# First mixture of a clustered-attention chain: weights bounded in place on VectorE, a fourth raw buffer, one block sum by accumulating DMA, one output block added by VectorE, and a new order of the steps

## The chip, the cores and the metric

The kernel runs on one core of one Trainium2 chip. The metric is device time in microseconds (us) of one execution of the whole program. All engine names are those of the profile: PE is TensorE (PEld its weight load), DVE VectorE, ACT ScalarE, POOL GpSimd, SP SyncE, which here only issues DMAs.

## The reference

Three layers run one after the other. The change touches the second.

```python
attn_out = _attn_ref(q, k, v, centroids)              # clustered attention, 2 x 8 heads, 768 x 64
x = attn_out.transpose(0, 2, 1, 3).reshape(1536, 512)
h = x @ w_in                                          # "first mixture": 512 -> 2048
g = h * (1.0 / (1.0 + np.exp(-h)))
x = g @ w_out                                         # 2048 -> 512
return _moe2_ref(x, w_gate, w1, w2)                   # 8 experts, weighted by a balanced gate
```

`w_in` and `w_out` come in float64, everything else that matters here in float32.

## The kernel before

**The first mixture** works in four stages `s`, each for 512 of the 2048 hidden columns. A stage has two layers, and each layer is one matrix product done as seven half-size block products with sums of blocks before and after. So a stage has 14 products: 0 to 6 are the A layer (x times w_in, PSUM tiles `l`), 7 to 13 the B layer (hidden values times w_out, tiles `y`). In the last stage the B layer is done plainly, as twelve output tiles (`ytile`, L803), because its results go straight to the third layer. Every float32 product is three PE passes: each operand is split into a rounded part `hi` and a rest `lo`.

For each product of a stage the other engines must do, in time:

- the weight factor: `mhi` (ACT casts a block of `win` or `win2` to `vh`, L150) and `mlo` (DVE subtracts, `vl`, L154). `vh` and `vl` alternate between two buffers, so those of product i can be written only when product i-2 is done;
- `aevac` (PSUM to the hidden block `h`: ACT copies or SiLU, L712 and L714; DVE adds, L716), `gsilu` (L721), `hsum` (DVE differences of hidden blocks, L753), `hhi` and `hlo` (ACT and DVE split the operand of a B product into `gh`, L759 and L763);
- `bevac` (B results): ACT copies PSUM to one of five output buffers (`rest`, `outx`, `stay`, L789), and POOL issues a DMA that adds the buffer to `acc1` (L791). The first stage's first result for each block is copied straight to `acc1`;
- `sums1`, `sum4`, `sum3`, `bsums1`, `bsum4`, `bsum3`: DVE sums of weight blocks.

**The weights** come in 32 pieces, numbered 4n + k; n = 2s is w_in and n = 2s + 1 is w_out of stage s. A piece is 512 KB: SP loads it raw into one of three buffers of pool `rawp` (`w_raw`, L86), as low and high 32-bit words. `w_steps` makes float32 of it: `wb` scales the low words (POOL, L107), `w0` scales the high words (ACT, L108; for one piece of each w_in set `wg` does that on POOL, L109), `w1` bounds the result (POOL, L110), `w2` and `w3` shift and join the bits (DVE, L111 and L112) and write the block of `win` or `win2`. In the last stage `w3` writes into the raw buffer, and `wh` and `wp2` split it into `woh` and `wol` (L113, L114). The next load into a buffer is issued when `w3` (in the last stage `wp2`) of the piece three places earlier has been issued.

**The order** is written out by hand. `put(s, u, f)` files a step under slot u of stage s; the main loop emits slot u's steps and then product u. Every engine works its own list strictly in that order, so a step that waits holds up all behind it on its engine, and POOL's list holds conversion steps and DMA issues together.

Of the kernel before, what the change touches and what calls it, by code (L numbers as in the profile page):

```python
# [18 lines left out]
P = 128  # L19
# [20 lines left out]
def attention_moe_kernel(ctx, tc, kq, vp, cent, w_in, w_out, w_gate, w1, w2, out):  # L40
# [31 lines left out]
    raws = {}  # L72
# [8 lines left out]
    def w_raw(n, k):  # L81

        raw = rawp.tile([P, 2 * FB], U32, name=f"wr{n}_{k}", tag="wr")
        shape = [P, 4, P, 2] if n % 2 == 0 else [P, 1, FB, 2]
        t = raw.rearrange("p (t f two) -> p t f two", t=shape[1], two=2)
        nc.sync.dma_start(out=t, in_=w_piece(n, k).bitcast(U32).rearrange("p t (f two) -> p t f two", two=2))  # L86
        raws[n, k] = t

    def w_steps(n, k, a=None):
# [13 lines left out]
        if 4 * n + k > 5:  # L103
            ts, v, top = nc.gpsimd.tensor_scalar, high.bitcast(F32), 122879.9921875 * 2.0**-112
            stt = nc.vector.scalar_tensor_tensor
            return dict(
                wb=lambda: ts(out=low, in0=low, scalar1=2.0**-29, scalar2=7.0, op0=ALU.mult, op1=ALU.min),  # L107
                w0=lambda: nc.scalar.activation(v, v, AF.Copy, scale=2.0**-112),  # L108
                wg=lambda: ts(out=v, in0=v, scalar1=2.0**-112, scalar2=1.0, op0=ALU.mult, op1=ALU.mult),  # L109
                w1=lambda: ts(out=v, in0=v, scalar1=-top, scalar2=top, op0=ALU.max, op1=ALU.min),  # L110
                w2=lambda: stt(out=low, in0=high, scalar=3, in1=low, op0=ALU.logical_shift_left, op1=ALU.bitwise_or),  # L111
                w3=lambda: stt(out=ai, in0=high, scalar=0x80000000, in1=low, op0=ALU.bitwise_and, op1=ALU.bitwise_or),  # L112
# [538 lines left out]
    wop = pool(rctx, "wop", bufs=1, side="right")  # L651
    mps = pool(rctx, "mps", bufs=6, space=PSUM)
# [4 lines left out]
    rest = wop.tile([P, 2048], F32, name="rest", tag="wol")  # L657
    wsum2 = rest[:, :512].rearrange("p (k f) -> p k f", k=2)
    outs = [rest[:, 512 + i * S : 512 + (i + 1) * S] for i in range(2)]
# [78 lines left out]
    BX = {1: (0, 1), 5: (0, 1), 6: (0, 1), 3: (1, 0), 7: (0, 0), 2: (1, 1), 4: (1, 1)}  # L738
# [3 lines left out]
    def bsums1():  # L742
        nc.vector.tensor_tensor(out=b21, in0=b21, in1=b22, op=ALU.add)
        nc.vector.tensor_tensor(out=wsum2, in0=b21, in1=b11, op=ALU.subtract)

    def bsum4():
        nc.vector.tensor_tensor(out=b21, in0=b12, in1=wsum2, op=ALU.subtract)

    def bsum3():
        nc.vector.tensor_tensor(out=b11, in0=b22, in1=wsum2, op=ALU.subtract)  # L750
# [26 lines left out]
    def bevac(s, j, pieces=PIECES):  # L777
# [4 lines left out]
        straight = s == 0 and p in (1, 5, 6, 4)  # L782
        if not straight and (s, j) not in moved:
# [15 lines left out]
    def ytile(s, t):  # L799
        c, d = CHUNKS[t // 4], t % 4  # L800
        ps = banks[t] = (mpy if t in (0, 1, 10, 11) else mps).tile([P, 512], F32, name=f"y{s}_{t}", tag="y" if t in (0, 1, 10, 11) else "s")
        def go(out, w, k, g, first=False, last=False):
            nc.tensor.matmul(out, lhsT=w[:, k, d * P : (d + 1) * P], rhs=g, start=first, stop=last, skip_group_check=True)  # L803
# [477 lines left out]
    def narrow(n, k, keys):  # L1281
# [3 lines left out]
        for key in keys.split():  # L1285
            quarters[n, k][key](*((wo_h[:, k : k + 1], wo_l[:, k : k + 1]) if key in ("wh", "wp2") else ()))
# [4 lines left out]
    LASTN = 2 * NS1 - 1  # L1291

    def bring(k):
        steps.pop(k + 4)
        nc.scalar.copy(win2[:, k : k + 1, :], raws[1, k][..., 1].bitcast(F32))
        w_raw(1 + (k + 3) // 4, (k + 3) % 4)

    X, Y, Z, V = (0, 1), (0, 0), (1, 0), (1, 1)
    for s in range(NS1):
        n, first, last = 2 * s + 1, s == 0, s == NS1 - 1  # L1300
        done = ("w2 w3 wh", "wp2") if last else ("w2 w3", "")
# [4 lines left out]
        def finish(u, k):  # L1306
            go(u, narrow, n, k, done[0])

        if not first:
            go(0, bevac, s - 1, 6)  # L1310
        go(0, mhi, s, 1)
        go(0, mlo, s, 1)
# [3 lines left out]
        else:  # L1316
            go(0, narrow, n - 1, 3, "w2 w3")
            go(0, sums1)
            go(0, narrow, n, 0, "w0 w1 wb")
        go(1, aevac, s, 0)  # L1320
        go(1, mhi, s, 2)
        go(1, mlo, s, 2)
        go(1, sum4)
        go(1, sum3)
        if first:
            go(1, split, 7, xb)
            go(1, narrow, n, 2, "w0 w1 wb")
        else:
            go(1, narrow, n, 1, "w0 w1 wb")
# [3 lines left out]
        if not first:  # L1333
            finish(2, 0)
            go(2, narrow, n, 2, "w0 w1 wb")
        go(2, gsilu, 2)
        go(3, aevac, s, 2)
        go(3, mhi, s, 4)
        go(3, mlo, s, 4)
        if not first:  # L1340
            if last:
                go(3, narrow, n, 0, done[1])
            finish(3, 1)
        else:
            go(3, split, 4, xd)
            go(3, narrow, n, 3, "w0 w1 wb")
        if last:
            go(3, ghi, 2)
        else:
            for m in range(2):  # L1350
                go(3, hhi, 0, m)
            for m in range(2):
                go(3, hlo, 0, m)
        go(4, aevac, s, 3)
        go(4, mhi, s, 5)
        go(4, mlo, s, 5)
        if last:
            go(4, narrow, n, 1, done[1])
        finish(4, 2)
        if last:  # L1360
            go(4, narrow, n, 2, done[1])
        if not first:
            go(4, narrow, n, 3, "w0 w1 wb")
        go(5, aevac, s, 4)
        go(5, mhi, s, 6)
        go(5, mlo, s, 6)
        go(5, gsilu, 7)
        finish(5, 3)
        go(6, aevac, s, 5)
        if last:  # L1370
            go(6, ghi, 7)
            go(6, narrow, n, 3, done[1])
# [16 lines left out]
        go(6, narrow, n + 1, 1, "w0 w1 wb")  # L1389
        go(7, bsums1)  # L1390
# [391 lines left out]
```

## Time and profile before

| | us |
|---|---|
| median of 3 runs | 1453.52 (1452.60 to 1454.64) |
| profiled execution, own time | 1451.86 |
| its span, first to last instruction | 1450.1 |
| around the span | 1.76 |

Busy shares of the span: PE 98%, PEld 88%, DVE 82%, ACT 70%, POOL 34%. The granted TensorE clock was 0.999 of full speed on average. In the page's 40 slices of 36 us, attention is the first six and a half, the first mixture lies from there to about the fourteenth, and the rest is the third layer. How to read it: a share over the whole span mixes three layers with different limits, and a PE row is longer (0.28 us) than the distance to the next one (0.12 us), since matmuls overlap; what the first mixture takes is therefore read from the starts of its products.

### The profile page before, as it was taken

To read this page: it belongs to the slowest core of one execution; us is meant where nothing else is said; L and a number is where in the kernel's file an instruction comes from. 1 tells how busy PE (TensorE), PEld (TensorE's weight loads), DVE (VectorE), ACT (ScalarE), POOL (GpSimd) and SP (SyncE) were. 2 spreads that over 40 slices of the span, in tenths; PEclk is the share of its full clock that TensorE was granted. 3 is DMA by queue.
4 is the path that set the end of the run, shared out by engine and by line. 5 is a ranking of instruction groups with operands and counts; after the bars stand their busy time and mean duration, and the time that the engine had idled before them with its cause. 6 is when DMAs were issued, how large, how long until landed. Compare 5 with 4: busy or idle time off the path is not lost.

```text
span 1450.1 us, 25558 instructions
## 1 busy us (share of the span) xinstructions
PE 1414.8 (98%) x9709; PEld 1279.2 (88%) x9709; DVE 1186.0 (82%) x1926; ACT 1018.1 (70%) x1974; POOL 486.6 (34%) x428
## 2 busy tenths in 40 slices
PE   8999999999997999999999999999999999999998
PEld 5777778877775889999999999999999999999998
DVE  7788887978776898988878778788787887887878
ACT  7777777766665367658577677786776867767765
POOL 6677754576864001121322322120211202212112
PEclk9999999999999999999999999999999999999999
DMA  7665520256574018486697897867957869569587
GB/s 221 184 170 156 172 65 29 52 160 123 146 164 120 1 36 176 83 158 147 134 184 136 164 156 143 167 108 124 162 95 145 137 115 171 98 120 167 89 153 131
DMA packets 141210, 190.87 MB, mean 132 GB/s; under 512 B 6816, under 2 KB 109216, under 8 KB 141088
## 3 DMA queue, kind: packets, MB, share of 16 engines
q0 software_dynamic: 88752, 100.94, 45.1%
q1 hardware_dynamic: 51648, 87.85, 19.4%
q8 instruction: 76, 1.25, 0.3%
q10 hardware_dynamic: 688, 0.46, 0.1%
q14 instruction: 46, 0.38, 0.1%
HBM read 65.36 MB, written 88.87 MB: 106 GB/s over the span
## 4 chain that ended last, share of the span: by engine, by line
PE 65%; DVE 1%; ACT 1%; issue 0%; DVEq 0%; ACTq 0%
PE b L685 27%; PE a L685 23%; PE b L1136 4%; PE q L1116 4%; PE r L1116 4%; PE y L803 2%; DVE acc L1217 1%; PE a L1130 0%; DVE al L848 0%; PE gl L1048 0%; ACT gh L726 0%; DVE h L845 0%; ACT acc L1234 0%; DVE h L1271 0%; DVE wfl L848 0%
## 5 line engine op out<-in xcount | busy, mean ns | idle before, releaser
L685 PE MATMUL b<-wfh,ah 128*128 128x256 f32 x1164 | 330.8, 284 | 0.0
L685 PE MATMUL b<-wfh,al 128*128 128x256 f32 x1164 | 329.2, 283 | 0.0
L685 PE MATMUL b<-wfl,ah 128*128 128x256 f32 x1164 | 329.1, 283 | 0.0
L1243 POOL DMA_DIRECT2D out_dram<-acc x87 | 126.5, 1720 | 533.6 <-ACT acc L1234 510.1
L1234 ACT ACTIVATE acc<-b,Pg 128x256 f32<-128x256 f32 x564 | 222.8, 540 | 6.2 <-PE b L1136 5.2
L685 PEld LDWEIGHTS b<-wfl,ah 128*128 128x128 f32 x1164 | 223.1, 192 | 0.0
L685 PEld LDWEIGHTS b<-wfh,ah 128*128 128x128 f32 x1164 | 222.9, 191 | 0.2
L685 PEld LDWEIGHTS b<-wfh,al 128*128 128x128 f32 x1164 | 223.0, 192 | 0.0
L685 PE MATMUL a<-xfl,wfh 128*128 128x512 f32 (+1 forms) x640 | 215.8, 337 | 0.0
L685 PE MATMUL a<-xfh,wfl 128*128 128x512 f32 (+1 forms) x640 | 215.5, 337 | 0.0
L685 PE MATMUL a<-xfh,wfh 128*128 128x512 f32 (+1 forms) x640 | 215.4, 337 | 0.0
L1169 ACT CAST ah<-h 128x768 fp32r<-128x768 f32 x160 | 134.6, 853 | 110.7 <-DVE h L1265 53.3
L1156 ACT COPY h<-a 128x512 f32<-128x512 f32 x192 | 113.9, 620 | 102.1 <-PE a L685 96.1
L848 DVE TENSOR_TENSOR al<-h,ah 128x768 fp32r<-128x768 f32 x160 | 151.3, 954 | 28.7 <-ACT ah L1169 23.4
L685 PEld LDWEIGHTS a<-xfh,wfl 128*128 128x128 f32 x640 | 120.9, 189 | 12.9
L685 PEld LDWEIGHTS a<-xfh,wfh 128*128 128x128 f32 x640 | 121.1, 189 | 11.6 <-issue 0.6
L685 PEld LDWEIGHTS a<-xfl,wfh 128*128 128x128 f32 x640 | 121.0, 189 | 10.4
L331 ACT ACTIVATE p<-s,m 128x768 f32<-128x768 f32 x96 | 86.7, 904 | 35.2 <-DVE m L322 30.7
L348 POOL TENSOR_SCALAR p<-p,rec 128x768 f32<-128x768 f32 x95 | 86.2, 920 | 51.5 <-DVE rec L336 39.4
L322 DVE TENSOR_REDUCE m<-s 128x1 f32<-128x768 f32 x96 | 90.0, 951 | 13.9 <-PE s L315 13.5
L845 DVE TENSOR_TENSOR h<-q,h 128x384 f32<-128x384 f32 x112 | 60.9, 554 | 35.1 <-PE q L1116 32.8
L848 DVE TENSOR_TENSOR wfl<-w0r,wfh 128x512 fp32r<-128x512 f32 x96 | 64.6, 688 | 28.9 <-ACT wfh L961 28.9
(281 smaller groups left out, 3498.6 us busy)
## 6 DMA issues: line engine op xcount, KB each, us to landing
out_dram<-acc POOLq DMA_DIRECT2D x91, 768.0 KB, 8.8
w0r<-in_w_dram SPq DMA_DIRECT2D x16, 1024.0 KB, 5.8
w1r<-in_w_dram SPq DMA_DIRECT2D x16, 1024.0 KB, 8.4
qk<-qk SPq DMA_DIRECT2D x45, 192.0 KB, 3.5
wr<-in_w_in_dram SPq DMA_DIRECT2D x16, 512.0 KB, 4.0
wr<-in_w_out_dram SPq DMA_DIRECT2D x16, 512.0 KB, 6.5
first_out<-acc POOLq DMA_DIRECT2D x10, 768.0 KB, 8.8
raw<-in_kq_dram SPq DMA_DIRECT2D x16, 384.0 KB, 4.1
```

The costliest lines, as they stand in the source:

```text
L322: nc.vector.tensor_reduce(out=m, in_=tiles[i]["s"][:, :S], axis=AX.X, op=ALU.max, negate=True)
L331: nc.scalar.activation(t["p"], t.pop("s")[:, :S], AF.Exp, bias=t.pop("m"), accum_out=chunks[c]["sum"][:, j, 0:1])
L348: e.tensor_scalar(out=p, in0=p, scalar1=chunks[c]["rec"][:, j : j + 1], scalar2=1.0, op0=ALU.mult, op1=ALU.mult)
L685: nc.tensor.matmul(ps[u][:, cols], lhsT=lf(i, k), rhs=rt(j, k), start=fresh and u not in opened, stop=k == 1 and q == 2, skip_group_check= ...
L845: e.tensor_tensor(out=out, in0=in0, in1=in1, op=op)
L848: e.tensor_tensor(out=lo, in0=x, in1=r(hi), op=ALU.subtract)
L1116: nc.tensor.matmul(ps, lhsT=quad_lhs(s, q, a, four), rhs=(x4 if four else xq)[b][:, XQ[q]], start=j == 0 and q in (1, 2, 5), stop=j == 2, ...
L1136: nc.tensor.matmul(ps[u][:, cols], lhsT=lf(i, k), rhs=rt(j, k), start=u not in opened, stop=k == 1 and q == 2, skip_group_check=True)
L1156: act.copy(bank(t, u), ps[u])
L1169: act.copy(hi, x)
L1234: act.mul(t[:, 2 * u + m], z[:, m], Pg[:, 6 * i + 2 * u + m, e : e + 1])
L1243: gps.dma_start(out=to, in_=t, accum_op=ALU.add)
```

## The change

- `w1` becomes a VectorE instruction (`clamp`) for all pieces but those of the last stage. `w0` writes the scaled high words straight into the place of `win` or `win2` (ACT for every piece; `wg` is gone), and `w1`, `w2`, `w3` work there; `wb` multiplies by a constant a little smaller and has no bound any more.
- A fourth raw buffer `rxp` takes the pieces 7, 11, 15, 19, 23 and 27, and loads are issued four pieces ahead. Piece 7 is loaded as soon as the buffer is there. `rest` becomes shorter, `wsum2` and the last `wol` block move.
- The signs of some sums change, so that one hidden block is a sum: `fourth` adds block (1,1) to block (0,1) by one accumulating DMA of 768 KB on POOL's queue. It takes the place of two DVE `hsum` instructions in each of the first three stages, and the last B product reads block (0,1).
- `bevac` of B product 12 (p = 2) is four DVE instructions that add PSUM to `acc1`, in place of four ACT copies and two DMAs.
- The lists are laid out anew: among others `mhi` stands ahead of the evacuations, the operand splits are interleaved by halves, and the conversion of the last piece of a w_in set (`w1 w2 w3`) follows directly before `sums1`.

```diff
+        raw = (rxp[0] if 4 * n + k in (7, 11, 15, 19, 23, 27) else rawp).tile([P, 2 * FB], U32, name=f"wr{n}_{k}", tag="wr")
...
-            ts, v, top = nc.gpsimd.tensor_scalar, high.bitcast(F32), 122879.9921875 * 2.0**-112
-            stt = nc.vector.scalar_tensor_tensor
+            ts, top = nc.gpsimd.tensor_scalar, 122879.9921875 * 2.0**-112
+            stt, clamp = nc.vector.scalar_tensor_tensor, ts if n == LASTN else nc.vector.tensor_scalar
             return dict(
-                wb=lambda: ts(out=low, in0=low, scalar1=2.0**-29, scalar2=7.0, op0=ALU.mult, op1=ALU.min),
-                w0=lambda: nc.scalar.activation(v, v, AF.Copy, scale=2.0**-112),
-                wg=lambda: ts(out=v, in0=v, scalar1=2.0**-112, scalar2=1.0, op0=ALU.mult, op1=ALU.mult),
-                w1=lambda: ts(out=v, in0=v, scalar1=-top, scalar2=top, op0=ALU.max, op1=ALU.min),
+                wb=lambda: ts(out=low, in0=low, scalar1=0.9374 * 2.0**-29, scalar2=1.0, op0=ALU.mult, op1=ALU.mult),
+                w0=lambda: nc.scalar.activation(a, high.bitcast(F32), AF.Copy, scale=2.0**-112),
+                w1=lambda: clamp(out=a, in0=a, scalar1=-top, scalar2=top, op0=ALU.max, op1=ALU.min),
...
+    def fourth():
+        nc.gpsimd.dma_start(out=hblk[0, 1], in_=hblk[1, 1], accum_op=ALU.add)
...
+        if p == 2:
+            for u, a, b, m, c in pieces:
+                z = to[:, m, c : c + b - a]
+                nc.vector.tensor_tensor(out=z, in0=ps[u][:, a:b], in1=z, op=ALU.add)
+            return
...
-            m = 4 * n + k + 3
-            if key == ("wp2" if n == LASTN else "w3") and 6 < m < 8 * NS1:
+            m = 4 * n + k + 4
+            m = {31: 32, 32: 31}.get(m, m)
+            if key == ("wp2" if n == LASTN else "w3") and m < 8 * NS1:
                 w_raw(m // 4, m % 4)
...
+        go(0, mhi, s, 1)
...
+            go(0, bevac, s - 1, 6)
+            go(0, narrow, n - 1, 3, "w1 w2 w3")
             go(0, sums1)
-            go(0, narrow, n, 0, "w0 w1 wb")
+        go(0, mlo, s, 1)
...
+        low(2, 0)
+        piece(2, 2, "w0")
+        piece(2, 3, "w0")
...
         go(2, gsilu, 2)
+        go(3, mhi, s, 4)
         go(3, aevac, s, 2)
...
-        go(11, hsum, V, V, X, m)
+        go(9, fourth)
```

How the lists moved, at the two places where stages meet or end. Rows are instructions in the order in which the engine works them; `wr_3_4825` and `wr_3_4511` are raw piece 27, `wr_0_4799`, `wr_1_4842`, `wr_2_4882` and `wr_3_5008` raw pieces 28 to 31 in the changed kernel.

ACT, from the third to the fourth stage, before: `vh_4876` and `vh_4922` are the weight parts of the fourth stage's products 0 and 1.

```order
L150 CAST vh_4876<-win 128x512
L108 ACTIVATE wr_3_4825<-wr_3_4825 128x512
L789 COPY rest<-y_2_1_4842 128x256 x2
L789 COPY rest<-y_2_0_4841 128x512
L789 COPY rest<-y_2_2_4843 128x512
L789 COPY outx<-y_1_1_4582 128x256
L789 COPY stay<-y_1_1_4582 128x256
L789 COPY outx<-y_1_0_4581 128x512
L789 COPY stay<-y_1_2_4583 128x512
L150 CAST vh_4922<-win 128x512
```

ACT at the same place in the changed kernel: `vh_4872` and `vh_4913` are the same two parts.

```order
L150 CAST vh_4872<-win 128x512
L109 ACTIVATE win<-wr_3_4511 128x4x128
L150 CAST vh_4913<-win 128x512
L799 COPY rest<-y_1_1_4583 128x256
L799 COPY outx<-y_1_1_4583 128x256
L799 COPY rest<-y_1_0_4582 128x512
L799 COPY outx<-y_1_2_4584 128x512
L109 ACTIVATE wr_0_4799<-wr_0_4799 128x512
```

Four copies (`rest<-y_2`) have left the list, and the other four stand behind the cast of product 1.

DVE at the same place in the changed kernel: the four additions to `acc`, the rest of the conversion with the bound (L110), the block sums (L135, L136) and the lo parts of products 0 and 1.

```order
L791 TENSOR_TENSOR acc_3466<-y_2_1_4846,acc_3466 128x256 x2
L791 TENSOR_TENSOR acc_3466<-y_2_0_4845,acc_3466 128x512
L791 TENSOR_TENSOR acc_3466<-y_2_2_4847,acc_3466 128x512
L154 TENSOR_TENSOR vl_4873<-win,vh_4872 128x512
L111 SCALAR_TENSOR_TENSOR wr_2_4472<-win,wr_2_4472 128x512
L112 SCALAR_TENSOR_TENSOR win<-win,wr_2_4472 128x4x128
L110 TENSOR_SCALAR win<-win 128x4x128
L111 SCALAR_TENSOR_TENSOR wr_3_4511<-win,wr_3_4511 128x512
L112 SCALAR_TENSOR_TENSOR win<-win,wr_3_4511 128x4x128
L135 TENSOR_TENSOR win<-win 128x2x256
L136 TENSOR_TENSOR wsum<-win 128x512
L154 TENSOR_TENSOR vl_4914<-win,vh_4913 128x512
```

Before, the additions were not in this list, L110 was POOL's, and the lo part of product 1 stood ahead of the conversion of piece 27.

ACT in the last stage of the changed kernel, behind the hi part of product 3 (`vh_5003`): `wr_3_5008` is the last raw piece, L723 the SiLU of a hidden block, `vh_5040` the hi part of product 4.

```order
L150 CAST vh_5003<-win 128x512
L109 ACTIVATE wr_2_4882<-wr_2_4882 128x512
L109 ACTIVATE wr_3_5008<-wr_3_5008 128x512
L723 ACTIVATE h_1_4960<-h_1_4960 128x768 x2
L150 CAST vh_5040<-win 128x512
L714 COPY h_6_5043<-l_1_0_4886 128x512
```

Before, the scaling of the last raw piece stood behind the hi part of product 5, directly ahead of that of product 6.

## Rows read from the trace of the kernel before

**Rows 1.** Windows, by stage: busy us of each engine (count), granted clock, DMA share, GB/s.

```profile
core 0: us, PE busy (x) PEld busy (x) DVE busy (x) ACT busy (x) POOL busy (x), PEclk, DMA share, GB/s
...
294.40:359.70 65.30, 60.57 (x336) 51.48 (x336) 54.19 (x69) 44.30 (x83) 47.34 (x29) 1.00 0.56 130
359.70:426.70 67.00, 61.58 (x336) 51.38 (x336) 53.37 (x69) 44.15 (x82) 48.45 (x31) 1.00 0.64 145
...
590.00:1430.00 840.00, 840.00 (x5959) 804.68 (x5958) 691.74 (x1096) 611.15 (x1210) 168.56 (x128) 1.00 0.76 137
```

**Rows 2.** Timeline of PE: first matmuls of products (start us, us, instruction, idle before).

```profile
233.18 0.50 PE L685 MATMUL l<-yh,vh 128*128 128x512 f32 x1
262.52 0.40 PE L685 MATMUL y<-gh,vh 128*128 128x256 f32 x2
276.28 0.40 PE L685 MATMUL y<-gh,vl 128*128 128x512 f32 x1
280.52 0.40 PE L685 MATMUL y<-gh,vl 128*128 128x512 f32 x1
294.47 0.50 PE L685 MATMUL l<-yh,vh 128*128 128x512 f32 x1 [0.50 <-ACT rest L789]
359.73 0.50 PE L685 MATMUL l<-yh,vh 128*128 128x512 f32 x1 [0.18 <-ACT outx L789]
426.74 0.51 PE L685 MATMUL l<-yh,vh 128*128 128x512 f32 x1 [0.18 <-ACT rest L789]
466.56 0.50 PE L803 MATMUL y<-gh,woh 128*128 128x512 f32 x1 [0.76 <-ACT gh L726]
```

**Rows 3.** Waits of PE from 233 to 502.1 us: total us, times, longest.

```profile
PE l L685 <- ACT vh L150: 10.1, 8, 2.4
PE y L685 <- DVE vl L154: 4.7, 5, 1.5
PE y L803 <- ACT gh L726: 2.2, 2, 1.5
```

**Rows 4.** Timeline of ACT: steps that waited, ahead of a late hi part.

```profile
298.54 0.68 ACT L108 ACTIVATE wr<-wr 128x512 f32<-128x512 f32 x1 [1.10 <-DMA wr<-in_w_out_dram]
...
363.71 1.35 ACT L789 COPY stay<-y 128x256 f32<-128x256 f32 x3 [2.65 <-DMA acc<-stay]
364.94 0.64 ACT L150 CAST vh<-win 128x512 fp32r<-128x512 f32 x1
```

**Rows 5.** Groups by line and form, 233 to 502.1 us: count, busy us, mean ns, idle before.

```profile
L110 POOL TENSOR_SCALAR wr<-wr 128x512 f32<-128x512 f32 x26 | 58.0, 2232 | 42.7 <-ACT wr L108 41.8
...
L753 DVE TENSOR_TENSOR h<-h,h 128x768 f32<-128x768 f32 x24 | 23.2, 1005 | 0.0
L716 DVE TENSOR_TENSOR h<-l,h 128x512 f32<-128x512 f32 x36 | 22.5, 681 | 0.0
L721 ACT ACTIVATE h<-h 128x768 f32<-128x768 f32 x24 | 18.9, 837 | 12.0 <-DVE h L716 12.0
```

**Rows 6.** Timelines of POOL and DVE: conversion steps side by side and alone, DMA issues.

```profile
312.85 2.31 POOL L107 TENSOR_SCALAR wr<-wr 128x512 uint32<-128x512 uint32 x1
...
313.21 1.14 DVE L111 SCALAR_TENSOR_TENSOR wr<-wr 128x512 uint32<-128x512 uint32 x1
321.50 0.69 DVE L111 SCALAR_TENSOR_TENSOR wr<-wr 128x512 uint32<-128x512 uint32 x1
...
427.46 1.77 POOL L791 DMA_DIRECT2D acc<-rest  x2 [3.71 <-ACT rest L789]
```

**Rows 7.** Instructions of line L120, a bound on VectorE in attention: ns min/median/max.

```profile
L120 DVE TENSOR_SCALAR u<-u x6: 418/418/548, 59.9 to 196.2; 128x512 f32<-128x512 f32 x6
```

**Rows 8.** DMA issues: KB each, median us to landing; last, raw weight loads from 425 to 465 us.

```profile
acc<-rest POOLq DMA_DIRECT2D x14, 384.0 KB, 6.8
out_dram<-acc POOLq DMA_DIRECT2D x91, 768.0 KB, 8.8
acc<-first_out SPq DMA_DIRECT2D x4, 768.0 KB, 13.6
...
DMA to landing us min/median/max: 3.6/8.5/9.9
```

More of the change, by code (lines that the diff above doesn't have):

```diff
@@ L656, in attention_moe_kernel @@
     win2 = wop.tile([P, 4, 512], F32, name="win2", tag="woh")
[L657 to L659 removed]
+    rest = wop.tile([P, 2, S], F32, name="rest", tag="wol")
+    wsum2 = wip.tile([P, 2, FB // 2], F32, name="wsum2", tag="ut")
+    outs = [rest[:, i] for i in range(2)]
     outs.append(pool(mctx, "outp", bufs=1).tile([P, S], F32, name="outx"))
@@ L802, in go @@
         def go(out, w, k, g, first=False, last=False):
-            nc.tensor.matmul(out, lhsT=w[:, k, d * P : (d + 1) * P], rhs=g, start=first, stop=last, skip_group_check=True)
+            nc.tensor.matmul(out, lhsT=w[k][:, 0, d * P : (d + 1) * P], rhs=g, start=first, stop=last, skip_group_check=True)
         if c < 2:
@@ L1300, in attention_moe_kernel, with piece, low @@
         n, first, last = 2 * s + 1, s == 0, s == NS1 - 1
-        done = ("w2 w3 wh", "wp2") if last else ("w2 w3", "")
+        mine = [k for k in range(4) if not first or k > 1]
         def go(u, f, *args):
             put(s, u, f, *args)
[L1306 to L1310, printed above, removed]
+        def piece(u, k, keys):
+            if k in mine:
+                go(u, narrow, n, k, keys)
+        def low(u, k):
+            if last:
+                go(u, narrow, n, k, "wp2")
         go(0, mhi, s, 1)
-        go(0, mlo, s, 1)
         if first:
@@ L1332, in attention_moe_kernel @@
         go(2, mlo, s, 3)
-        if not first:
-            finish(2, 0)
-            go(2, narrow, n, 2, "w0 w1 wb")
+        low(2, 0)
+        piece(2, 2, "w0")
+        piece(2, 3, "w0")
+        piece(2, 1, "w1")
+        piece(2, 3, "wb")
         go(2, gsilu, 2)
+        go(3, mhi, s, 4)
         go(3, aevac, s, 2)
-        go(3, mhi, s, 4)
         go(3, mlo, s, 4)
[L1340 to L1344, printed above, removed]
+        if first:
             go(3, split, 4, xd)
-            go(3, narrow, n, 3, "w0 w1 wb")
+        piece(3, 1, "w2 w3")
+        piece(3, 2, "w1 w2 w3")
         if last:
-            go(3, ghi, 2)
+            go(3, narrow, n, 1, "wh")
+            go(3, narrow, n, 2, "wh")
+        low(3, 1)
+        go(4, mhi, s, 5)
+        go(4, aevac, s, 3)
+        piece(4, 3, "w1 w2 w3")
+        go(4, mlo, s, 5)
+        low(4, 2)
+        if last:
+            go(4, narrow, n, 3, "wh")
+            go(4, ghi, 2)
+            go(4, glo, s, 2)
         else:
             for m in range(2):
[L1351 to L1363, printed above, removed]
+                go(4, hhi, 0, m)
+                go(4, hlo, 0, m)
+        go(5, mhi, s, 6)
         go(5, aevac, s, 4)
-        go(5, mhi, s, 6)
         go(5, mlo, s, 6)
+        low(5, 3)
+        if not last:
+            go(5, narrow, n + 1, 0, "w0")
         go(5, gsilu, 7)
-        finish(5, 3)
         go(6, aevac, s, 5)
```

107 lines of the change are left out of this document (58 added, 49 removed).

## The prediction

> **What bounds the kernel now.** I read the windows by stage first, then the starts of products on PE, then PE's waits, then the lists of the engines that PE waits for. From 590 to 1430 us PE is busy 840.00 of 840.00 us, at a granted clock of 1.00 [rows 1]. So nothing behind the first mixture can hide time that the mixture saves: each microsecond saved there moves the end by one. Inside the mixture a floor comes from the starts of products [rows 2]. The first A layer took 262.52 - 233.18 = 29.34 us for seven products. Two consecutive B products started 280.52 - 276.28 = 4.24 us apart, and seven of them take 29.68. An unstalled stage is 59.0 us. The real stages took 61.29, 65.26 and 67.01 us (the four starts), 2.3, 6.2 and 8.0 over the floor. The last stage's A layer took 466.56 - 426.74 = 39.82, 10.5 over 29.34. The plain output tiles waited another 2.2 [rows 3]. Together **29.2 us are lost**, and that is the most the change can win. The waits that the trace lists are fewer (10.1 on ACT's hi parts, 4.7 on DVE's lo parts, 2.2 on `gh` [rows 3]), because each stall also hides some of the overlap between matmul rows; I therefore count by starts.
>
> Why the hi parts are late stands in ACT's list: at 363.71 a `stay` copy waited 2.65 us for the DMA that empties an output buffer, at 298.54 a `w0` waited 1.10 us for a raw load, and the cast of the next hi part comes right behind [rows 4]. POOL spends 2.23 us on each bound [rows 5] and up to 2.31 on each `wb` [rows 6], 16 of them a stage, some 36 us, and the block sums wait at the end of that list. DVE is busy 54.2 and 53.4 us of the stages of 65 and 67 us [rows 1]: near the floor, but below it.
>
> **The change part by part**, for stages of 59.0 us.
>
> *POOL* loses eight bounds a stage (8 x 2.23 = 18 us), keeps eight `wb`, and is no longer late for the block sums in the first three stages. In the last stage it keeps its bounds.
>
> *DVE* gains eight bounds of one operand. The same form in attention took 418 ns, 548 at most [rows 7]; the two-operand conversion step took 0.69 [rows 6] and is the upper end. I take 0.42, since it is the same operation on the same tile shape: 3.4 us. It gains four additions from PSUM, two of 512 columns at 0.68 [rows 5] and two of 256, between 0.34 and 0.68; I take 0.42, some 2.2 in all. It loses two differences of 1.0 [rows 5]. That is 54.2 + 3.4 + 2.2 - 2.0 = **57.8 us of 59.0**. A step beside POOL takes 1.14 us in place of 0.69 [rows 6]; with 16 POOL steps a stage at most 7.2 us of DVE's time is such lengthening, and with eight at most 3.6, so up to 3.6 comes back: 54.2 to 57.8. DVE stays under the floor, but with little room.
>
> *ACT* loses four copies of about 0.45 (a third of 1.35 [rows 4]) and with them two output buffers to wait for; of the other four copies the hi part of the next stage's product 1 now stands ahead. It gains one `w0`, 0.68 [rows 4]. The 2.65 us wait thus no longer delays a hi part.
>
> *Stage boundaries.* Product 12 ends 4.2 us before the next stage starts. DVE then works 2.2 (additions), 0.69 (lo of product 0), 1.4 (two steps of the third piece), 0.42 + 1.4 (the last piece), 1.4 (block sums) and 0.69 (lo of product 1): 8.2 us, ready 4.0 after the start, for a product due at 4.2. One or two steps lengthened by 0.45 make it late, so I leave 1.0 lost at each of three boundaries, and 1.5 of the first stage's 2.3, whose first pieces hardly change: **4.5 us**.
>
> *Loads.* With a fourth buffer a load is issued one piece earlier; a load took 3.6 to 9.9 us [rows 8], so the 1.10 us wait goes.
>
> *The accumulating DMA.* It moves 768 KB, as the two result DMAs of 384 KB that go do. POOL issues it in 0.9 us (half of 1.77 [rows 6]) at product 9, and ACT's cast for the last B product wants it three products later, 12.6 us: 11.7 are left. The nearest rows are 6.8 us for an accumulation of 384 KB, 8.8 for 768 KB from the same queue without one, and 13.6 for 768 KB from SP's queue [rows 8]. I take 8.8, same queue and size: nothing waits. By 13.6 each of three stages would lose 1.9, 5.7 us.
>
> *The last stage* sets the rest. Let T be the start of its product 2, 8.4 us after the stage's start. ACT does a cast (0.6) and four copies (1.8), POOL two DMA issues (1.8 [rows 6]), `wb` of piece 29 and the bound of piece 28 (2.2 each): T + 0.2. DVE then needs 1.4 for `w2 w3`, 2.0 for three additions, 0.69 for the lo of product 3, 0.69 for `wp2`: T + 5.0. Only then SP loads piece 31, 3.6 us at best [rows 8]: T + 8.6. ACT's list now holds `w0` of that piece (0.68) ahead of two SiLUs (0.84 each [rows 5]) and the hi part of product 4 (0.64 [rows 4]): T + 11.6, for a product due at T + 8.4, so 3.2 are lost. Piece 31 goes on through POOL (`wb`, two bounds: T + 15.2) and DVE (1.4, the lo of product 5, `wp2`, two splits of 1.0, three additions, the lo of product 6, T + 22.7), for a product 6 due at T + 20.0: 2.7 more. The output tiles I leave 0.4. **6.3 us.**
>
> *Sum*: 29.2 - 4.5 - 6.3 = 18.4. The profiled execution took 1451.86, so 1433.5 there. The median of the runs stands 1.66 above that execution, so 1435.1 as a median.
>
> **The rivals.**
>
> *DVE becomes the bound.* If POOL's eight remaining steps fall where DVE is busiest, nothing comes back and DVE needs 57.8 us in lists with waits of their own. For it: the boundary list has 0.2 us of room. Against it: stages of 65 us had DVE at 54.2 [rows 1] and PE waited twice as long for ACT as for DVE [rows 3]. Two to four microseconds more in three stages give 1441 to 1447. Chance 0.17.
>
> *DVE waits for whole POOL steps.* A conversion step that starts beside POOL would wait, not for 0.45, but for the end of a 2.2 us step, on average 1.1. Eight steps a stage at 1.1 - 0.45 are 5.2 on top of 57.8, 63 for a floor of 59.0, 4.0 lost in each of three stages, and the same once more where the boundary list is late: about 1448. Against it stands the row of 1.14 us, which began inside a POOL step and ended inside it [rows 6]. Chance 0.05.
>
> The Trainium skill, page "SBUF — State Buffer", section "SBUF: two separate sides", states this rule: VectorE and GpSimd share a port pair as "an exclusive lock, not a bandwidth split", and the loser blocks for the whole instruction, a VectorE step with two SBUF inputs among them. It speaks against putting more on VectorE beside POOL; the trace's 1.14 against 0.69 shows a slowing and not a block, so I go by the trace.
>
> *The accumulating DMA lands late*, and the kernel ends slower. ACT works its list in order, so a cast that waits for this DMA holds the copies and the next hi parts behind it. It decides from 11.7 us after the issue; each microsecond beyond costs three. To end slower by more than a measurement of this kernel can tell from no change (0.2%, 2.9 us), it must eat the gain of 18.4 and 2.9 more, 7.1 a stage, and so land after 18.8 us. For it: DMA engines are 0.56 to 0.64 busy in these stages [rows 1], weight loads run beside it, and no row shows an accumulation of this size between two buffers of the core. Against: 13.6 is the longest near row [rows 8]. Chance 0.07, and 0.03 of it slower.
>
> *The loads gain nothing.* Buffers come free by `w3` or `wp2` on DVE, and where DVE is the later engine the fourth buffer is only filled and not needed sooner; then each boundary keeps a wait of up to 2.65 [rows 4], 8 us, 1443. The last stage has the same in its sharpest form: piece 31 landing in 9.9 in place of 3.6 costs 6.3, 1441. Chance 0.11.
>
> **How the numbers follow.** My forecast has 0.60, the rivals 0.17, 0.05, 0.07 and 0.11. Faster by over 0.2% (below 1450.6) are the forecast, nearly all of the first and the last rival, and half of the rest: 0.91. Within 0.2% lie the second rival's upper half and a DMA near 18 us: 0.05. Slower: 0.04. The range begins where the boundaries lose nothing and the last stage half of what I gave it (29.2 - 1.5 - 3.1 = 24.6, 1428.9 as a median; I take 1428.5) and ends inside the DVE rival, at 1446; with that some 2 in 10 are left out.
>
> **What would show it.** Right: products 4.2 us apart through the first three stages and stage starts 59 to 60.5 us apart; PE's waits on hi parts nearly gone there; POOL's bound only four times, DVE's at about 0.42; the largest stall before product 4 of the last stage, with ACT's `w0` of piece 31 waiting for a raw load. Wrong: stages of 62 us or more with PE waiting for lo parts (DVE is the bound), DVE rows of over 2 us beside POOL (whole steps), ACT's cast of block (0,1) waiting for a DMA at product 12 (late accumulation), or the last stage losing 12 instead of 6.

## The result, and the profile after

The changed kernel takes **1431.52 us** (median of 4 runs, 1430.89 to 1432.09); the kernel before, run beside it, 1454.08 (1452.60 to 1454.72). The ratio is 0.9846, 95% interval 0.9829 to 0.9863: faster by 22.6 us. The forecast was 1435.1, in a range of 1428.5 to 1446.0, so the direction and the range held; the time is 3.6 us under the forecast, and the gain of 22.6 us stands against 18.4 forecast.

The starts of the stages on PE in the changed kernel's trace answer to [rows 2]: the first matmul of the four A layers, of the output tiles and of the third layer.

```profile
234.37 0.50 PE L687 MATMUL l<-yh,vh 128*128 128x512 f32 x1
...
294.20 0.40 PE L687 MATMUL l<-yh,vh 128*128 128x512 f32 x1
...
353.92 0.40 PE L687 MATMUL l<-yh,vh 128*128 128x512 f32 x1
...
413.77 0.39 PE L687 MATMUL l<-yh,vh 128*128 128x512 f32 x1
...
448.97 0.40 PE L813 MATMUL y<-gh,woh 128*128 128x512 f32 x1
...
482.26 0.39 PE L687 MATMUL a<-xfh,wfh 128*128 128x512 f32 x1
```

| stretch, us | before | after | over the floor after |
|---|---|---|---|
| stage 1 | 61.29 | 59.83 | 0.8 |
| stage 2 | 65.26 | 59.72 | 0.7 |
| stage 3 | 67.01 | 59.85 | 0.8 |
| last stage, A layer | 39.82 | 35.20 | 5.9 |
| output tiles | 35.41 | 33.29 | |
| sum | 268.79 | 247.89 | |

The mixture gives 20.9 us. The span went from 1450.1 to 1430.1, 20.0 less: in this execution attention ended 1.2 later (the first start was 233.18), and the third layer took 0.3 less. The first start lies between 233.1 and 235.0 in the eleven traces of the changed kernel and its variants, so nothing is made of that 1.2. The medians are 22.6 apart because the profiled execution of before (1451.86, granted clock 0.999) is a quick one: the executions of before that were run beside the experiments took 1451.88 to 1457.28 us at granted clocks from 0.999 down to 0.993.

The windows by stage show the same and what the engines did in it; they answer to [rows 1]. Columns: stretch, length, busy us (count) of PE, PEld, DVE, ACT and POOL, granted clock, DMA share, GB/s.

```profile
234.37:294.20 59.83, 59.25 (x337) 51.78 (x337) 50.17 (x75) 45.30 (x79) 8.48 (x10) 1.00 0.32 79
294.20:353.92 59.72, 59.15 (x337) 51.67 (x336) 54.58 (x80) 43.15 (x78) 16.25 (x19) 1.00 0.60 142
353.92:413.77 59.85, 59.40 (x338) 51.78 (x336) 54.05 (x79) 43.07 (x78) 19.09 (x23) 1.00 0.73 161
413.77:448.97 35.20, 30.62 (x169) 25.75 (x168) 27.07 (x39) 21.58 (x38) 13.32 (x10) 1.00 0.59 155
```

PE is busy all but 0.5 us of a stage. POOL fell from 47 and 48 us to 16 and 19. DVE hardly rose, 54.6 and 54.1 us against 54.2 and 53.4, though it took over the bounds and the additions; its share of the shorter stages went up from 0.83 and 0.80 to 0.91 and 0.90.

All that PE still waits for in the first mixture (the timeline of PE, rows with idle time before them; the last bracket is the idle time and its releaser):

```profile
299.36 0.39 PE L687 MATMUL l<-yh,vl 128*128 128x256 f32 x1 [0.57 <-DVE vl L154]
...
358.88 0.39 PE L687 MATMUL l<-yh,vl 128*128 128x256 f32 x1 [0.36 <-DVE vl L154]
...
419.21 0.39 PE L687 MATMUL l<-yh,vl 128*128 128x256 f32 x1 [0.86 <-DVE vl L154]
...
433.56 0.73 PE L687 MATMUL l<-yf,vh 128*128 128x512 f32 x2 [1.80 <-ACT h L714]
...
438.61 0.38 PE L687 MATMUL l<-yh,vh 128*128 128x256 f32 x1 [0.58 <-ACT h L714]
439.44 0.39 PE L687 MATMUL l<-yh,vl 128*128 128x256 f32 x1 [0.34 <-DVE vl L154]
445.13 0.50 PE L687 MATMUL l<-yf,vl 128*128 128x512 f32 x1 [1.00 <-DVE vl L154]
```

Ahead of them stands one wait of 0.58 in the first stage. The first three are the lo part of product 1 at the stage boundaries; the rest lies in the last stage. The waits for hi parts, eight of them in the A layers [rows 3], are gone.

The groups of the changed instructions, 234 to 483 us, answer to [rows 5 to 7] (line, engine, count, busy us, mean ns, idle before):

```profile
L108 POOL TENSOR_SCALAR wr<-wr 128x512 uint32<-128x512 uint32 x24 | 21.0, 874 | 73.0 <-DMA wr<-in_w_in_dram 39.1 <-DMA wr<-in_w_out_dram 17.2 <-DVE win L112 5.7
...
L110 DVE TENSOR_SCALAR win<-win 128x512 f32<-128x512 f32 x22 | 10.6, 483 | 0.0
...
L110 POOL TENSOR_SCALAR wr<-wr 128x512 f32<-128x512 f32 x4 | 8.7, 2196 | 0.2
```

The bound costs 0.48 us on DVE and 2.20 on POOL. The first row is the surprise: `wb` (now line 108) fell from 2.2 to 0.87 us. And the last stage's largest stall shows in ACT's list:

```profile
423.33 0.62 ACT L150 CAST vh<-win 128x512 fp32r<-128x512 f32 x1
423.85 0.68 ACT L109 ACTIVATE wr<-wr 128x512 f32<-128x512 f32 x1
430.38 0.68 ACT L109 ACTIVATE wr<-wr 128x512 f32<-128x512 f32 x1 [5.85 <-DMA wr<-in_w_out_dram]
430.95 1.56 ACT L723 ACTIVATE h<-h 128x768 f32<-128x768 f32 x2
432.42 0.60 ACT L150 CAST vh<-win 128x512 fp32r<-128x512 f32 x1
432.93 1.55 ACT L714 COPY h<-l 128x512 f32<-128x512 f32 x3
```

`w0` of piece 31 waits 5.85 us for its load, and the SiLUs, the hi part of product 4 (432.42) and the copies of product 2 stand behind it, as the prediction had it. PE's wait of 1.80 us before product 4 (433.56) ends with the first of these copies, which comes right behind the hi part.

### The profile page after: what moved, and what is told of

Read it like the earlier page. It is cut to its first block, busy times and chain, and to the rows that moved or that the text cites. A ratio compares the mean times of both kernels' runs of the same rounds, so it can differ in the third digit from the quotient of the medians.

```text
span 1430.1 us, 25524 instructions
## 1 busy us (share of the span) xinstructions
PE 1410.6 (99%) x9708; PEld 1280.8 (90%) x9709; DVE 1187.5 (83%) x1954; ACT 1013.3 (71%) x1965; POOL 396.3 (28%) x400
## 4 chain that ended last, share of the span: by engine, by line
PE 66%; DVE 1%; issue 0%; ACT 0%; DVEq 0%; ACTq 0%
PE b L687 28%; PE a L687 23%; PE b L1146 4%; PE q L1126 4%; PE r L1126 4%; PE y L813 2%; DVE acc L1227 1%; PE a L1140 0%; DVE al L858 0%; PE l L687 0%; PE gl L1058 0%; DVE h L855 0%; ACT acc L1244 0%; DVE h L1281 0%; DVE wfl L858 0%
```

## Experiments

The theories: **1**, the change won by taking work off POOL; **2**, it won by the order of the lists; **3**, ScalarE's waits for output buffers were the cause; **4**, VectorE has no room, so what is put on it shows. Times are medians, ratios are to the kernel before, run beside (1454.24, 1452.84 and 1453.35 us in the three groups that follow).

### What POOL's work is worth

**wb_min.** `wb` with the old constants and the minimum.

```diff
-                wb=lambda: ts(out=low, in0=low, scalar1=0.9374 * 2.0**-29, scalar2=1.0, op0=ALU.mult, op1=ALU.mult),
+                wb=lambda: ts(out=low, in0=low, scalar1=2.0**-29, scalar2=7.0, op0=ALU.mult, op1=ALU.min),
```

> The changed kernel, but wb is again a multiply and a minimum (2^-29, 7.0) on GpSimd. In the changed kernel's trace a wb takes 0.87 us, in the one before 2.19. Theory 1 (GpSimd's relief is what the change won by): the row goes back to about 2.2 us, GpSimd works some 10 us more in each stage, more VectorE steps run beside it, and the lists where stages meet get later: 1433 to 1436 us. Theory 2 (the order of the lists is what counts, GpSimd has time to spare): the row goes back to 2.2 us and the time stays at 1431 to 1432.5.

Measured: 1433.37 us, ratio 0.9852 (0.9839 to 0.9866). The row goes to 2209 ns. The time is 1.9 us above the changed kernel's, with the intervals overlapping, and the three stages start at 294.17, 353.88 and 413.77, as in the changed kernel: only the last stage is 0.3 us longer. So the median falls into theory 1's range, but its mechanism, later lists where stages meet, does not show: in the new order some 10 us more of POOL work a stage are hidden.

**pool_bounds.** All bounds on POOL, `wb` cheap.

```diff
-            stt, clamp = nc.vector.scalar_tensor_tensor, ts if n == LASTN else nc.vector.tensor_scalar
+            stt, clamp = nc.vector.scalar_tensor_tensor, ts
```

> The changed kernel, but all bounds on GpSimd; wb stays cheap. Theory 1: the last piece's bound stands behind the two DMA issues of the last product's copies, starts some 3 us after the stage's start and takes 2.2 us; the block sums and the lo part of product 1 behind it on VectorE come some 4 us late at each of three boundaries: 1440 to 1447 us. Theory 2: the new order gives GpSimd enough time, only the longer step itself shows (2.2 - 0.4 us at each of three boundaries): 1432 to 1437 us.

Measured: 1448.85 us, ratio 0.9957 (0.9944 to 0.9971), 17.3 us more than the changed kernel and above both expectations. Stages 2 and 3 take 62.81 and 69.31 us, the last A layer 40.86. The timeline of POOL at the boundary to stage 3, which starts at 356.39, shows why:

```profile
357.96 1.21 POOL L108 TENSOR_SCALAR wr<-wr 128x512 uint32<-128x512 uint32 x1
359.21 0.91 POOL L801 DMA_DIRECT2D acc<-stay  x1
359.81 1.21 POOL L801 DMA_DIRECT2D acc<-rest  x1
361.10 1.91 POOL L110 TENSOR_SCALAR win<-win 128x512 f32<-128x512 f32 x1
```

and DVE behind it:

```profile
363.05 0.69 DVE L111 SCALAR_TENSOR_TENSOR wr<-win,wr 128x512 uint32<-128x512 uint32 x1 [3.33 <-POOL win L110]
```

The last piece's bound stands behind a `wb` and two DMA issues, DVE waits 3.33 us for it, and PE then waits 3.27 for the lo part of product 1. An earlier bound does the same to product 0, whose hi part comes 1.65 us late. In the first three stages all of PE's waits stand at products 0 and 1; none stands in mid-stage. So a bound is on the path where it stands close ahead of a weight part or of the block sums.

The waits are not all of the loss. PE behind the wait of 3.27 us:

```profile
367.18 0.38 PE L687 MATMUL l<-yh,vl 128*128 128x256 f32 x1 [3.27 <-DVE vl L154]
...
368.48 0.63 PE L687 MATMUL l<-yh,vh 128*128 128x512 f32 x1
368.91 0.63 PE L687 MATMUL l<-yl,vh 128*128 128x512 f32 x1
...
371.89 0.40 PE L687 MATMUL l<-yh,vl 128*128 128x512 f32 x1
372.12 0.40 PE L687 MATMUL l<-yh,vh 128*128 128x512 f32 x1
```

From 368.48 on, matmuls of the same shape start 0.43 us apart, from 371.89 on 0.23: in between the granted clock is at the lower of its two levels (1.2 in place of 2.4 GHz). Its mean is 0.95 over stage 3 and 0.87 over the last A layer; in the changed kernel it is 1.00 in both. By these means TensorE lost 0.05 x 69.31 = 3.5 us and 0.13 x 40.86 = 5.3 us of its work, an estimate: some 9 of the 17.3 us are the clock behind the waits, and not the waits themselves. No rule for when it falls comes out of these runs: a PE wait of 3.19 us in the last stage of act_copies, further down, left it at 1.00.

**pool_both.** Both edits.

> The changed kernel with the bounds on GpSimd and wb with the minimum, so GpSimd has as much conversion work as before. Theory 1: nearly all of the gain goes, 1445 to 1453 us. Theory 2: 1434 to 1440 us.

Measured: 1455.16 us, ratio 1.0005 (0.9996 to 1.0014), above both expectations: the whole gain is gone, with the new order, the fourth buffer, the accumulating DMA and VectorE's additions all in place. PE's waits for lo parts come to 17.1 us in seven waits, the longest 6.3. The granted clock falls here too, to 0.97, 0.95 and 0.92 in stages 2 and 3 and the last A layer (65.45, 69.78 and 42.88 us), again some 9 us by the same estimate. With the bounds on POOL the cheap `wb` is worth 6.3 us (1455.2 to 1448.9), without them 1.9. Theory 2 alone falls.

**b_wb_only.** The kernel before with the new constants in `wb` and nothing else (the first diff in reverse, line 107).

> The kernel before, with one thing of the change alone: wb multiplies twice (0.9374 x 2^-29, then 1.0) and has no minimum. Both theories expect the row to fall from 2.19 to about 0.9 us. Theory 1: GpSimd's bounds and DMA issues come earlier, and 3 to 8 us of the 22 are won by this alone: 1446 to 1451 us. Theory 2: ScalarE's order and its waits for output buffers set the time: 1452 to 1455 us.

Measured: 1446.63 us, ratio 0.9942 (0.9929 to 0.9954): a third of the gain by a change of two constants and an operation. The row is 876 ns, from 2188. (Its trace has a granted clock of 0.97 in stage 3 and 0.95 in the last A layer; both are 1.00 in the trace of before.)

**b_dve_bounds.** The kernel before with the cheap `wb` and the bounds on VectorE.

```diff
-                w1=lambda: ts(out=v, in0=v, scalar1=-top, scalar2=top, op0=ALU.max, op1=ALU.min),
+                w1=lambda: nc.vector.tensor_scalar(out=v, in0=v, scalar1=-top, scalar2=top, op0=ALU.max, op1=ALU.min),
...
-            go(0, narrow, n, 0, "w0 w1 wb")
+            go(0, narrow, n, 0, "w0 wb")
...
-            go(0, narrow, n - 1, 3, "w2 w3")
+            go(0, narrow, n - 1, 3, "w1 w2 w3")
```

(and likewise for the other pieces)

> The kernel before with its own order of lists, but wb multiplies twice and the bounds are VectorE's (directly ahead of w2, in the raw buffer). Three buffers, five output buffers and all block sums as before. Theory 1 in its strong form (GpSimd's relief alone does it): 1433 to 1438 us. Theory 1 with the order (GpSimd's relief and the new order need each other): with the order of before, ScalarE still waits for output buffers and loads ahead of the hi parts, 1440 to 1446 us. Theory 2 (order alone): no better than the cheap wb alone, 1446 us or more.

Measured: 1445.03 us, ratio 0.9940 (0.9927 to 0.9954), no different from the cheap `wb` alone by the intervals. PE still waits six times for hi parts, 4.7 us, and stage 3 takes 65.11. The time falls into the expectation that relief and order need each other. So neither half does it: the order without POOL's relief gives nothing (pool_both), POOL's relief in the old order 8 us, the two with the smaller parts 22.6.

### The smaller parts

**act_copies.** B product 12 goes out by ScalarE and two DMAs again.

```diff
-        if p == 2:
-            for u, a, b, m, c in pieces:
-                z = to[:, m, c : c + b - a]
-                nc.vector.tensor_tensor(out=z, in0=ps[u][:, a:b], in1=z, op=ALU.add)
-            return
```

> The changed kernel, but the result of B product 12 goes out as before: four ScalarE copies into output buffers and two accumulating DMAs, in place of four VectorE additions. Theory 1 (GpSimd's relief is what the change won by): VectorE gets some 2 us back at each boundary, GpSimd gets two issues of 0.9 us more ahead of the last bounds, and ScalarE's copies now stand behind the hi part; the sum is small either way, 1430 to 1434 us. Theory 3 (waits for output buffers on ScalarE were the cause): the waits come back, 1436 to 1442 us.

Measured: 1440.17 us, ratio 0.9904 (0.9887 to 0.9921): 8.7 us, theory 3's size (6.9 in the mixture of the profiled execution). The timeline of ACT ahead of stage 3, which starts at 353.74:

```profile
349.02 0.36 ACT L794 COPY rest<-y 128x256 f32<-128x256 f32 x1
353.32 0.37 ACT L794 COPY outx<-y 128x256 f32<-128x256 f32 x1 [3.93 <-DMA acc<-outx]
...
359.51 1.35 ACT L794 COPY stay<-y 128x256 f32<-128x256 f32 x3 [2.06 <-DMA acc<-stay]
```

A copy waits 3.93 us for the DMA that empties its output buffer. PE now waits for the copy itself, not for a hi part: product 0 of the next stage starts 1.62 late, and product 1 has another 1.76 (releasers `outx` and `stay`). The additions on DVE take 1.95 us and no buffer.

**dve_sums.** Two DVE additions in slot 11 in place of the accumulating DMA (`hsum` takes the operation as a further argument).

```diff
-        go(9, fourth)
...
         go(11, bevac, s, 3)
+        for m in range(2):
+            go(11, hsum, X, X, V, m, ALU.add)
```

> The changed kernel with two VectorE additions of 0.95 us (in slot 11) in place of the accumulating DMA. VectorE is busy 54.2 of 59.8 us of a stage in the changed kernel's trace. Theory 1: 1.9 us more fit into the 5 idle us: 1431 to 1433 us. Theory 4 (VectorE is at its bound): all of it shows in three stages, 1436 to 1438 us.

Measured: 1435.03 us, ratio 0.9866 (0.9848 to 0.9884): 3.5 us, between the two. Of 1.9 us put on DVE, 1.0 to 1.4 show in each of three stages (60.87, 60.80 and 61.22). DVE is idle 5 us of a stage, but in the stretch from the last B products to the block sums it has next to nothing to spare: PE waits 0.73 us for the lo part of product 13, then 0.67 to 1.12 for that of product 1.

**three_bufs.** Three raw buffers, loads three pieces ahead, the early load of piece 7 gone, one `wb` moved (slot 7 to 13).

```diff
-        raw = (rxp[0] if 4 * n + k in (7, 11, 15, 19, 23, 27) else rawp).tile([P, 2 * FB], U32, name=f"wr{n}_{k}", tag="wr")
+        raw = rawp.tile([P, 2 * FB], U32, name=f"wr{n}_{k}", tag="wr")
...
-            m = 4 * n + k + 4
-            m = {31: 32, 32: 31}.get(m, m)
+            m = 4 * n + k + 3
```

> The changed kernel with three raw buffers and loads three pieces ahead; the wb of each w_in set's last piece had to move from slot 7 to slot 13, since its load is issued later. Theory 1: the loads were seldom what was late, but the last piece's w0 and wb now stand close behind their load, and a wait there costs what it lasts: 1431 to 1436 us. Rival (the fourth buffer carries much of the gain): 1438 to 1445 us, with ScalarE's w0 waiting for raw loads at the boundaries.

Measured: 1440.03 us, ratio 0.9902 (0.9886 to 0.9918): 8.5 us, the rival's size. ACT's `w0` (line 109) waits twelve times for a load (its idle time by releaser, us and times):

```profile
  DMA wr<-in_w_out_dram: 21.2, 9
  DMA wr<-in_w_in_dram: 5.5, 3
```

against two waits in the changed kernel:

```profile
  DMA wr<-in_w_out_dram: 7.7, 2
```

Behind the longest one, 4.86 us in stage 3, stands again the hi part of product 4. The granted clock of the last A layer is 0.96 here, under 2 of the 8.5 us. The prediction's rival that the loads gain nothing is wrong.

**late_fourth.** The accumulating DMA in slot 11.

```diff
-        go(9, fourth)
...
+        go(11, fourth)
         go(11, bevac, s, 3)
```

> The changed kernel with the accumulating DMA issued two products later (slot 11 in place of 9, some 8.4 us). It landed 5.8 to 8.6 us after its issue. If the cast of the last B product's operand, 12.6 us after the start of product 9, is what it must meet: 8.4 + 0.9 + 7.7 = 17.0, 4.4 us late in each of three stages, 1441 to 1446 us. Rival (ScalarE's list has more room there, since the cast is only needed a product later): 4.2 us of the lateness are covered, 1431 to 1435 us.

Measured: 1442.35 us, ratio 0.9918 (0.9905 to 0.9931): 10.8 us. The timeline of ACT ahead of product 13 in stage 2:

```profile
351.67 1.56 ACT L764 CAST gh<-h 128x768 fp32r<-128x768 f32 x2 [6.04 <-DMA h<-h]
353.14 0.61 ACT L150 CAST vh<-win 128x512 fp32r<-128x512 f32 x1
353.66 0.36 ACT L799 COPY outx<-y 128x256 f32<-128x256 f32 x1
```

The cast waits for the DMA, and a hi part and the copies wait behind it. The windows of stages 2 and 3 (columns as above):

```profile
294.86:360.53 65.67, 61.08 (x338) 52.79 (x336) 55.41 (x82) 43.01 (x78) 16.37 (x19) 0.97 0.62 143
360.53:425.65 65.12, 60.76 (x337) 52.80 (x336) 54.05 (x79) 43.12 (x78) 18.57 (x21) 0.97 0.67 148
```

They take some 5.6 us more than in the changed kernel: PE waits 3.73 and 4.36 us for the copies, and the clock of 0.97 takes up to 2 us more of each. The DMA was issued 8.0 and 7.2 us later in these two stages, measured from the stage's start, and landed after 9.3 and 9.5 us. Stage 1 takes 59.83, as before the edit, but it is no test: POOL has nothing else to do between the two slots there, and its DMA was issued 39.6 us after the stage's start in both kernels and landed after 5.8. In the changed kernel the three land in 5.8, 7.7 and 8.6 us, and nothing waits; in stage 2 the DMA is issued at 333.64 and the cast starts at 344.67, 11.0 us later. So the deadline is near the 11.7 us of the prediction, and the slack is real but not wide. That the total fell into the range of the first expectation is in part luck: two stages lost, not three, and the clock made up for part of the third.

### What is left, and a faster version

**lo_early.** The lo part of product 1 ahead of the last piece's conversion.

```diff
             go(0, bevac, s - 1, 6)
+            go(0, mlo, s, 1)
             go(0, narrow, n - 1, 3, "w1 w2 w3")
             go(0, sums1)
-        go(0, mlo, s, 1)
+        if first:
+            go(0, mlo, s, 1)
```

> The changed kernel with one step moved: at each stage boundary the lo part of product 1 stands ahead of the conversion of the last piece (bound, w2, w3) and of the block sums, not behind them. In the changed kernel's trace PE waits 0.57, 0.36 and 0.86 us for this part at the three boundaries. If that is all that is late there: the three waits go, 1429.5 to 1430.5 us. Rival (the block sums become late by the 0.7 us that the lo part now takes ahead of them, and product 2 waits): 1431 to 1433 us.

Measured: 1431.45 us, ratio 0.9845 (0.9832 to 0.9859), no gain. The three waits are gone, and stage 2 runs at 58.89 us, the floor. Stage 3 gives it back, 61.25 us (columns as in the windows above):

```profile
293.07:351.96 58.89, 58.89 (x337) 51.62 (x336) 55.26 (x81) 42.99 (x78) 15.02 (x18) 1.00 0.61 144
351.96:413.21 61.25, 59.85 (x337) 51.54 (x336) 53.66 (x79) 43.14 (x78) 18.59 (x23) 1.00 0.71 157
```

by one new wait on PE:

```profile
375.05 0.39 PE L687 MATMUL l<-yh,vl 128*128 128x256 f32 x1 [1.40 <-DVE vl L154]
```

The time falls into the rival's range, but its mechanism is neither of the two expectations: not the block sums, but the lo part of product 5. In this trace DVE converts three pieces in a row ahead of it, behind the hi part of product 4, and that behind a `w0` that waits for its load; the same pattern as in the last stage. That this load sets the time there was not tried by itself. The last A layer, 35.26 us, gains nothing either: it starts without its 0.86 us wait, but its granted clock is 0.95.

**last_stage.** In the last stage alone, `w0` of piece 31 and its conversion go behind the parts that PE waits for, the second hidden block's split behind the lo part of product 6, and the bounds to VectorE.

```diff
-            stt, clamp = nc.vector.scalar_tensor_tensor, ts if n == LASTN else nc.vector.tensor_scalar
+            stt, clamp = nc.vector.scalar_tensor_tensor, nc.vector.tensor_scalar
...
-        piece(2, 3, "w0")
+        if not last:
+            piece(2, 3, "w0")
...
         go(3, mlo, s, 4)
+        if last:
+            piece(3, 3, "w0")
...
-        piece(4, 3, "w1 w2 w3")
+        if not last:
+            piece(4, 3, "w1 w2 w3")
         go(4, mlo, s, 5)
         low(4, 2)
+        if last:
+            piece(4, 3, "w1 w2 w3")
...
             go(4, ghi, 2)
-            go(4, glo, s, 2)
...
         low(5, 3)
+        if last:
+            go(5, glo, s, 2)
```

> The changed kernel with the last stage laid out anew: w0 of piece 31, which waits 5.85 us for its load, stands behind the hi and the lo part of product 4; its bound, w2 and w3 behind the lo part of product 5; the split of the second hidden block behind the lo part of product 6; and the bounds of the last four pieces on VectorE. If the load was in the way of the lists only: the last A layer falls from 35.2 to 30 to 31.5 us, the output tiles wait for their operands up to 1.5 us: 1426.5 to 1429 us. Rival (what is won goes to the output tiles, whose operands are ready no sooner): 1430 to 1432 us.

Measured: 1428.35 us, ratio 0.9824 (0.9811 to 0.9838), runs from 1427.71 to 1428.87 against 1430.89 to 1432.09. The last A layer takes 30.0 us (412.91 to 442.92), 5.2 less; the output tiles take 34.5 in place of 33.3. The first expectation holds; which of the four moves did how much was not tried.

**both.** The two diffs above together.

> lo_early and last_stage together. If each takes away its own waits they add up: 1425 to 1427.5 us. Rival (the later work takes it back): not under 1429 us.

Measured: **1427.25 us** (1426.93 to 1427.90), ratio 0.9817 (0.9804 to 0.9831): the quickest version here, 4.3 us under the changed kernel and within the first expectation. Its interval overlaps that of last_stage, so that lo_early adds to it is not shown. Its windows, stage 3 and the last A layer:

```profile
353.52:414.13 60.61, 59.57 (x337) 51.62 (x336) 53.98 (x79) 42.93 (x78) 17.50 (x22) 1.00 0.70 159
414.13:443.54 29.41, 29.41 (x169) 25.75 (x168) 26.40 (x41) 20.47 (x36) 4.49 (x6) 1.00 0.69 180
```

The last A layer stands at the floor of 29.3. ACT there (timeline) no longer holds anything behind the load:

```profile
424.87 1.57 ACT L723 ACTIVATE h<-h 128x768 f32<-128x768 f32 x2
426.80 0.62 ACT L150 CAST vh<-win 128x512 fp32r<-128x512 f32 x1 [0.37 <-PE l L687]
427.32 1.55 ACT L714 COPY h<-l 128x512 f32<-128x512 f32 x3
430.56 0.69 ACT L109 ACTIVATE wr<-wr 128x512 f32<-128x512 f32 x1 [1.68 <-DMA wr<-in_w_out_dram]
```

The load lands when it did (430.56 against 430.38), but the SiLUs, the hi part and the copies come first.

## Why the prediction was right, point by point

**What bounds the kernel.** Right. What the mixture saved (20.9 us in the traces) moved the end by 20.0, and the rest of the program did not change by more than its own scatter.

**POOL.** The direction was right, and pool_both shows it: give POOL its work back and the whole gain goes. The size was wrong in one term: "keeps eight `wb`", priced at 2.31 us from the row of before [rows 6]. They took 0.87 us. The diff changed the second operation from a minimum to a multiply, and the prediction read that as the same instruction. In the new order the error was cheap (wb_min: 1.9 us, not clear of its noise), in the old one the same edit is worth 7.6.

**DVE.** Forecast 54.2 to 57.8 us of 59.0; it was 54.6 and 54.1, at the low end. The bounds were 0.48 on average (0.42 the median), as taken; the four additions 1.95 in place of 2.2. So some 3.4 us of 57.8 came back. The forecast expected that of fewer POOL steps beside DVE's; that POOL's `wb` is short now is not the reason, since wb_min, with `wb` at 2.2 us and POOL busy 27.3 and 29.4 us, has DVE at 54.3 and 54.0. Whether the bounds' leaving POOL or the new order gave it back stays open. A step is still lengthened beside POOL, by some 0.45 us (the longest bound on DVE took 0.88), and no single step of 512 columns reached 1.2 us, in wb_min neither; the rival of whole POOL steps is out, and the rule of the Trainium skill cited beside it (page "SBUF — State Buffer", section "SBUF: two separate sides") does not show in these rows.

**ACT and its output buffers.** Right that no hi part waits behind them any more. act_copies shows the missing part: without VectorE's additions the wait returns, not to a hi part but to the next stage's product 0.

**Stage boundaries.** Forecast 1.0 lost at each, by the lo part of product 1; measured waits 0.57, 0.36 and 0.86. The first stage kept 0.8 where 1.5 was left. Together with the third boundary 4.5 forecast, about 3.2 measured.

**Loads.** Underpriced: "so the 1.10 us wait goes". three_bufs puts 8.5 us on the fourth buffer (with one `wb` moved), because the new order lets hi parts stand behind `w0`s that wait for a load. In the changed kernel itself two such waits are left, 1.83 us in stage 3, behind which PE waits for nothing, and the 5.85 of the last stage.

**The accumulating DMA.** Taken 8.8 us with 11.7 at hand; it landed in 5.8 to 8.6. late_fourth confirms the deadline and the rival's mechanism in stages 2 and 3, some 5.6 us each with the clock. That each microsecond beyond costs three was not tried, since stage 1's DMA was no later there.

**The last stage.** Right in place and mechanism. Forecast 6.3 beside its boundary, of it 0.4 in the output tiles; measured about 5.0 and none. `wp2` of piece 28 was done 3.4 us behind the start of product 2 (423.26), not 5.0, so piece 31 was loaded earlier (it was issued at 426.71 and landed 3.6 later, the low end of [rows 8], as taken). The short `wb` explains little of it: with the old one (wb_min) the stage is 0.3 longer.

**The sum.** Of 29.2 us lost before, 10.8 were to stay and 8.3 stayed, so the forecast gain was 2.5 too small: 1.3 at the stage boundaries and 1.3 in the last stage. The forecast counted what would stay lost and not what each part wins; that is why a `wb` priced 1.4 us too high and a buffer priced some 7 us too low hardly moved it. In the profiled execution attention took 1.2 of the gain back and the third layer gave 0.3. The other 2.0 of the 3.6 us lie between executions: the forecast put the median 1.66 above the profiled one, as in the kernel before, and the changed kernel's median lies 0.4 below its own profiled execution (1431.9).

**What stays open.** The single undos (`wb` 1.9, bounds 17.3, copies 8.7, sums 3.5, buffer 8.5) add up to 39.9 us for a gain of 22.6. Without what the lower clock took in pool_bounds and three_bufs, some 10 us by the estimates above, they still add up to 29 to 30. The parts are not additive, and no split of the gain among them is right. The new order with all parts undone at once was not tried, nor what holds stage 3 at 60.6 us in the quickest version, where PE's one wait is 1.04 us for the lo part of product 5.

## What to carry to other kernels

Before pricing work that moves between engines, ask which wait it stands ahead of: with the bounds back on POOL, PE's waits in the first three stages stood only where a bound came behind DMA issues and close ahead of weight parts or block sums, and the kernel took 17 us more. Read the granted clock beside each long wait of PE: about half of those 17 us was TensorE at its lower clock behind the waits. In a list that an engine works in order, a step that waits for a load goes behind everything that does not need it; last_stage, which did this with three other moves, won 3.2 us, and in both, which keeps its moves, the load landed no later. Treat an edit of an operation's constants and kind as a new instruction, and look for a row of that kind before carrying the old price over.

## What the runs showed of the hardware that was not expected

On the same 128x512 uint32 tile, POOL's multiply with a minimum took 2.19 us and its multiply with a multiply 0.87 (both kernels, and turned round in wb_min and b_wb_only). Its float bound (maximum and minimum) took 2.20, and the same bound on VectorE 0.48. A row of before hinted at it: `wg`, two multiplies on POOL, took 1.36 us.

```profile
L109 POOL TENSOR_SCALAR wr<-wr x3: 1357/1372/1374, 269.0 to 400.0; 128x512 f32<-128x512 f32 x3
```

(Instructions of line 109 of the kernel before: ns min/median/max, first and last start, forms.) The Trainium skill, page "GPSIMD Engine Reference", section "4.1 Engine selection", calls one-input elementwise work on GpSimd roughly line-rate; by that the minimum would cost no more than the multiply. These runs speak against it: the price depended on the operations, by 2.5 times (the constants changed with them in `wb`, so the minimum alone was not tried).

An accumulating DMA of 768 KB between two buffers of the core landed in 5.8 us in the stage with a DMA share of 0.32 and in 7.7 and 8.6 in those with 0.60 and 0.73. The share alone does not set it: in late_fourth it took 9.3 and 9.5 us in stages with 0.62 and 0.67.
